# Linear-attention and SwiGLU block, forward and backward: loading the first x tile in two halves and transposing the eighth by DMA

## The chip, the cores and the metric

The kernel runs on one core of one Trainium2 chip. The metric is the device time of one execution in microseconds (us). A NeuronCore has TensorE (PE, matrix products), VectorE (DVE), ScalarE (ACT), GpSimd (POOL) and SyncE (SP); DMAs are issued from the queues of SP, ACT and POOL. "PEld" in a profile is TensorE's weight load, which overlaps its products.

## The reference

With S = 2048 tokens, D = 640, H = 32 heads of 20 and F = 1728, the reference computes the forward pass below and the gradients of its output to x and to all weights:

```
n   = layernorm(x);  q, k, v = split(n @ wqkv)
phi = t -> where(t > 0, t + 1, exp(t)) + 1e-6
o   = (phi(q) (phi(k)^T v)) / (phi(q) . sum(phi(k)) + 1e-6)      per head
h   = x + o @ wo
out = h + (silu(ln(h) @ w_gate) * (ln(h) @ w_up)) @ w_down
```

Only the beginning matters for the change: the layer norm of x and the products for k and q, followed by phi.

## The kernel before

The tokens are cut into 16 tiles of 128 (`ST` = 16). The first stage, which the change concerns, goes over the tiles t = 0 to 15. For each tile DVE computes the row statistics (`ln1_stats`, L268), POOL makes 1/sqrt(var + eps) from them (`ln_rstd`, L137, with two operations, L139 and L140), and DVE writes the normalised copy `xn` (`ln1_xn`, L281). The first `NC` = 3 tiles are only centred (`ln1_centre`, L277), and ACT multiplies by the scale when it reads the product. The product needs `xn` transposed, as `xnT`. For tiles t < `XD` = 8, TensorE transposes it into PSUM in five blocks of 128 columns (`ln1_tr` for tiles 0 and 1, `ln1_tr1` for 2 to 7), and ACT or DVE copies it to SBUF (`copies`, `copy1`; DVE for the tiles in `BY_V`, where they go through `copy1`). For the tiles from `XD` on, SP issues a transposing DMA from `xn` into `xnT` (L378), three tiles ahead of use.

`kq_mm(t, which)` (L299) is the product of tile t for k (`which` = 0) or q (1): ten matmuls of 320 columns, then two reads by ACT, an exp into `pk` or `pqa` and a relu into a ring `rr`. `phi` (L313) joins two tiles of these on DVE in two operations. The tile of PSUM comes from a pool of four slots that all such tiles share by rotation (tag "mm"). A transposed tile is asked for in `between`, after the product's first piece: in the first three products the five blocks of k are taken in `PIECES`, three and then two, so that work can begin on the first three.

Around this, the kernel keeps TensorE busy from the beginning with dummy products of the identity with itself (`warm`, L339: 37 ahead of tile 0's transposes and 8 behind them). Loads are paced: the first statistics release the loads of x tiles 2 and 3 and of w_q (`load_2`), the first copy of tile 0 releases the rest of x and a transposed load of w_down (`load_3`).

The order of this stage is written out by hand: L335 opens a `manual_schedule` that lists all five engines, so each executes its instructions in the order of the program text. On SP this order is: x tile 0, two pieces of w_k, the paced loads, then for each t the transposing DMA of tile t + 3 where there is one, and what the table `queue` (L328) names for t: transposed loads of the output gradient `dh2T` (the first 512 rows at t = 4), and stores of `xnT`, `pk` and `pqa` to DRAM for the backward pass. ACT's queue carries x tile 1. `dh2T` is first used after the products of the stage. Later stages list fewer engines in their `manual_schedule`, and there a planner orders the others by estimated times.

In the loop from L369 the order on DVE for a tile t is: statistics of later tiles, `ln1_xn(t + 3)` where it is for DMA, copies of transposed tiles, then `phi`, then `ln1_xn(t + 2)` for the tiles that TensorE transposes, and at t = `XD` - 4 = 4 the eighth tile's, `ln1_xn(7)`.

The later stages are long sequences of products: key-value sums, attention, the SwiGLU products, and the backward pass.

Of the kernel before, what the change touches and what calls it, by code (L numbers as in the profile page):

```python
# [9 lines left out]
BF16 = mybir.dt.bfloat16  # L10
# [5 lines left out]
P = 128  # L16
# [4 lines left out]
def kernel(  # L21
# [8 lines left out]
    nc = tc.nc  # L30
# [4 lines left out]
    DT = D // P  # L35
# [13 lines left out]
    x_v = A_x.rearrange("b (t p) d -> p (b t) d", p=P)  # L49
# [5 lines left out]
    const = ctx.enter_context(tc.tile_pool(name="const", bufs=1))  # L55
    dram = ctx.enter_context(tc.tile_pool(name="dram", bufs=1, space=bass.MemoryType.DRAM))
    psum = ctx.enter_context(tc.tile_pool(name="psum", bufs=4, space=bass.MemoryType.PSUM))
# [5 lines left out]
    def mm(name):  # L63

        return psum.tile([P, 2, 512], FP32, name=name, tag="mm")

    def row(ps):
        return ps[:, :, :320]

    def half(ap):  # L70
        return ap.rearrange("p (c n) -> p c n", c=2)
# [122 lines left out]
    x_tm = [strips.tile([P, 8, D], BF16, name="x_tm", tag="S") for _ in range(2)]  # L194
# [6 lines left out]
    def load_x(eng, t0, t1):  # L201
        return eng.dma_start(out=x_tm[t0 // 8][:, t0 % 8:(t1 - 1) % 8 + 1, :], in_=x_v[:, t0:t1, :])

    load_x(nc.sync, 0, 1)
    load_x(nc.scalar, 1, 2)
    w_k = A_wqkv[:, D:2 * D].rearrange("(k p) n -> p k n", p=P)
    w_q = A_wqkv[:, 0:D].rearrange("(k p) n -> p k n", p=P)
# [3 lines left out]
    def wait_for(on, dmas):  # L211
        info = mybir.DependencyInfo(mybir.DependencyClass.Sync, mybir.DependencyReason.DATA)
        for dma in dmas:
            tc.add_manual_dep(dma.ins, on.ins.name, info, reason="paced")
# [7 lines left out]
    def load_3():  # L222
        for t0 in range(4, ST, 2):
            yield load_x(nc.sync, t0, t0 + 2)
        yield load_wdT(wdT, 0)
# [11 lines left out]
    with tc.manual_schedule(engines={EngineType.Pool}):  # L237
        ident = const.tile([P, P], BF16, name="ident")
        make_identity(nc, ident[:])
        nhalf = const.tile([P, 4], FP32, name="nhalf")  # L240
        nc.vector.memset(nhalf[:], -0.5)
        ones = const.tile([P, P], BF16, name="ones")
        nc.vector.memset(ones[:], 1.0)
    mask = const.tile([P, 160], BF16, name="mask")
    zb = const.tile([P, D], BF16, name="zb")
    dzb = const.tile([P, D], BF16, name="dzb")
# [13 lines left out]
    xn = big.tile([P, ST, D], BF16, name="xn", tag="B")  # L260
    xnT = big.tile([P, ST, DT, P], BF16, name="xnT", tag="B")
    pk = big.tile([P, ST, D], BF16, name="pk", tag="B")
    pqa = big.tile([P, ST, D], BF16, name="pqa", tag="B")
    NC = 3
    XD = 8
    BY_V = (1, 2, 3)

    def ln1_stats(t):  # L268
        st6 = small.tile([P, 2, 6], FP32, name="st6", tag="st6")
        for ci, (n0, n1) in enumerate(NCH):  # L270
            st = nc.vector.bn_stats(out=st6[:, ci, :], in_=x_tm[t // 8][:, t % 8, n0:n1])
            if t == 0 and ci == 0:
                wait_for(st, load_2())
        nc.vector.bn_aggr(out=mv1[:, t, :], in_=st6[:].rearrange("p a b -> p (a b)"))
        ln_rstd(mv1[:, t:t + 1, :], rstd1, t, 1)

    def ln1_centre(t, c0=0, c1=D):  # L277
        nc.vector.tensor_scalar(out=xn[:, t, c0:c1], in0=x_tm[t // 8][:, t % 8, c0:c1], scalar1=mv1[:, t, 0:1],
                                scalar2=None, op0=ALU.subtract)

    def ln1_xn(t):  # L281
        nc.vector.tensor_scalar(out=xn[:, t, :], in0=x_tm[t // 8][:, t % 8, :], scalar1=mv1[:, t, 0:1],
                                scalar2=rstd1[:, t:t + 1], op0=ALU.subtract, op1=ALU.mult)

    def ln1_tr(t):
        tp = psum.tile([P, 2, 2 * 512], BF16, name="ps_t", tag="mm")
        for c, (k0, k1) in enumerate(((0, 3), (3, DT))):
            for kt in range(k0, k1):
                nc.tensor.transpose(tp[:, c, (kt - k0) * P:(kt - k0 + 1) * P], xn[:, t, kt * P:(kt + 1) * P], ident[:])
        return [(slice(k0, k1), tp[:, c, :(k1 - k0) * P].rearrange("p (k c) -> p k c", c=P))  # L290
                for c, (k0, k1) in enumerate(((0, 3), (3, DT)))]

    def ln1_tr1(t):
        tp = psum.tile([P, D], BF16, name="ps_t", tag="mm")
        for kt in range(DT):
            nc.tensor.transpose(tp[:, kt * P:(kt + 1) * P], xn[:, t, kt * P:(kt + 1) * P], ident[:])
        return tp[:].rearrange("p (k c) -> p k c", c=P)

    def kq_mm(t, which, between=None, pieces=((0, DT),)):  # L299
        dst, w0 = ((pk, D), (pqa, 0))[which]  # L300
        ps = mm("ps_kq")
        for k0, k1 in pieces:
            for ci, (n0, n1) in enumerate(NCH):
                for k in range(k0, k1):
                    nc.tensor.matmul(ps[:, ci, :320], lhsT=xnT[:, t, k, :], rhs=wqk[:, k, w0 + n0:w0 + n1],  # L305
                                     start=(k == 0), stop=(k == DT - 1))
            if between and k0 == 0:
                between()
        sc = rstd1[:, t:t + 1] if t < NC else 1.0
        nc.scalar.activation(out=half(dst[:, t, :]), in_=row(ps), func=ACT.Exp, scale=sc)  # L310
        nc.scalar.activation(out=half(rr[:, 2 * which + t // 2 % 2, t % 2, :]), in_=row(ps), func=ACT.Relu, scale=sc)
# [21 lines left out]
    PIECES = ((0, 3), (3, DT))  # L333

    with tc.manual_schedule(engines={EngineType.PE, EngineType.DVE, EngineType.Activation, EngineType.Pool, EngineType.SP}):  # L335

        ps = mm("ps_warm")

        def warm(n):  # L339
            for _ in range(n):  # L340
                nc.tensor.matmul(ps[:, 0, :P], lhsT=ident[:], rhs=ident[:], start=True, stop=True)  # L341

        def copies(t, eng_copy):
            for sl, src in ln1_tr(t):
                c = eng_copy(out=xnT[:, t, sl], in_=src)
                if t == 0 and sl.start == 0:
                    wait_for(c, load_3())

        def copy1(t):
            (nc.vector.tensor_copy if t in BY_V else nc.scalar.copy)(out=xnT[:, t], in_=ln1_tr1(t))  # L350

        warm(37)
        ln1_stats(0)
        ln1_centre(0, 0, 3 * P)
        ln1_centre(0, 3 * P, D)
        copies(0, nc.scalar.copy)
        warm(8)
        ln1_stats(1)
        ln1_centre(1)
        kq_mm(0, 0, lambda: copies(1, nc.vector.tensor_copy), PIECES)  # L360
        ln1_stats(2)
        ln1_centre(2)
        kq_mm(1, 0, None, PIECES)
        ln1_stats(3)
        kq_mm(0, 1, lambda: copy1(2), PIECES)
        phi(0, 0)
        ln1_xn(3)
        kq_mm(1, 1)
        for t in range(2, ST):  # L369
            if t == 2:  # L370
                ln1_stats(4)
            if t == 4:
                ln1_stats(t + 3)
            if 4 <= t < ST - 4:
                ln1_stats(t + 4)
            if XD <= t + 3 < ST:
                ln1_xn(t + 3)
                nc.sync.dma_start_transpose(out=xnT[:, t + 3], in_=xn[:, t + 3, :])  # L378
            kq_mm(t, 0, (lambda: copy1(t + 1)) if t + 1 < XD else None)
            if t == 2:  # L380
                ln1_stats(5)
            if t == 3:
                ln1_stats(6)
            if t == ST - 1:
                phi(0, t - 1, 1)
            kq_mm(t, 1)
            if t == 3:
                phi(1, 0)
            elif t == ST - 1:
                last_phi = phi(0, t, 1)  # L390
            elif t > 3:
                phi(t % 2, t - 2 - t % 2)
            if t + 2 < XD - 1:
                ln1_xn(t + 2)
            if t == XD - 4:
                ln1_xn(t + 3)
            if ST - NC - 1 <= t < ST - 1:
                ln1_xn(t - ST + NC + 1)
            for f, *a in queue.get(t, ()):
                f(*a)  # L400
# [71 lines left out]
    with tc.manual_schedule(engines={EngineType.PE, EngineType.DVE, EngineType.SP, EngineType.Pool}):  # L472
# [25 lines left out]
        for i in range(DT):  # L498
            ps = mm("ps_y")
            for ci, (n0, n1) in enumerate(NCH):  # L500
                for t in range(ST):
                    nc.tensor.matmul(ps[:, ci, :320], lhsT=xn[:, t, i * P:(i + 1) * P], rhs=pk[:, t, n0:n1],  # L502
                                     start=(t == 0), stop=(t == ST - 1))
# [36 lines left out]
        for i in range(DT):  # L540
            if i % 2 == 0 and i > 0:
                dm(1)
            ps = mm("ps_w2t")
# [15 lines left out]
        for t in range(ST + 2):  # L559
            if t < ST:  # L560
                xr = wk("h1")
                ps = mm("ps_a")
                for ci, (n0, n1) in enumerate(NCH):
                    for i in range(DT):
                        nc.tensor.matmul(ps[:, ci, :320], lhsT=pqsT[:, i, t * P:(t + 1) * P], rhs=W2[:, i, n0:n1],  # L565
                                         start=(i == 0), stop=(i == DT - 1))
# [42 lines left out]
    with tc.manual_schedule(engines={EngineType.SP}):  # L609
# [14 lines left out]
        for g in range(4):  # L624
# [4 lines left out]
            for t in range(0, ST, 2):  # L629
                pg = mm("pg")  # L630
                for c in range(2):
                    for kt in range(DT):
                        nc.tensor.matmul(pg[:, c, :w], lhsT=hnT[:, kt, (t + c) * P:(t + c + 1) * P], rhs=wg[:, kt, 0:w],  # L633
                                         start=(kt == 0), stop=(kt == DT - 1))
                pu = mm("pu")
                for c in range(2):
                    for kt in range(DT):
                        nc.tensor.matmul(pu[:, c, :w], lhsT=hnT[:, kt, (t + c) * P:(t + c + 1) * P],  # L638
                                         rhs=wg[:, kt, w:2 * w], start=(kt == 0), stop=(kt == DT - 1))
# [108 lines left out]
    with tc.manual_schedule(engines={EngineType.SP, EngineType.Pool}):  # L748
# [20 lines left out]
        for t in range(ST + LAG_C):  # L769
            if t < ST:  # L770
# [6 lines left out]
                ps = mm("ps_dhn")  # L777
# [32 lines left out]
            ps = mm("ps_dp")  # L810
# [14 lines left out]
    with tc.manual_schedule(engines={EngineType.SP, EngineType.DVE}):  # L825
# [27 lines left out]
        for i in range(DT):  # L853
            ps = gts.pop(i, None)
            if ps is None:
                ps = mm("ps_gt")
# [57 lines left out]
        ps = mm("ps_dzb")  # L914
# [11 lines left out]
        for t in range(ST + LAG):  # L926
            if t in (2, 3):
                dwqk(0, t + 1)
            if t < ST:
# [5 lines left out]
                ps = mm("ps_dk")  # L935
# [25 lines left out]
            ps = mm("ps_dxn")  # L961
            for ci, (n0, n1) in enumerate(NCH):
                for k, (lhs, rhs) in enumerate(((dqT, wqkvT[:, 0:5]), (pkT, WV2), (dkT, wqkvT[:, 5:10]))):
                    for i in range(DT):
                        nc.tensor.matmul(ps[:, ci, :320], lhsT=lhs[:, i, :], rhs=rhs[:, i, n0:n1],  # L965
                                         start=(k == 0 and i == 0), stop=(k == 2 and i == DT - 1))
# [127 lines left out]
```

## Time and profile before

| what | before |
|---|---|
| time, median of 4 runs | 812.68 us (812.61 to 812.73) |
| time of the profiled execution | 811.96 us |
| its span | 810.2 us |
| TensorE clock granted | 1.0 |
| first dummy product on TensorE | 1.56 us |
| first product of tile 0 (L305) | 6.52 us |
| last product of the k and q stage ends | about 52.2 us |
| transposing DMAs of x tiles (L378) | 8, the first issued at 24.38 us |

Times within the profile count from the start of the span. A line of the timeline gives start and length in us, the engine (with a q for its queue, which issues DMAs), the source line, the operation, what it writes and reads, and in brackets the idle time before it and what ended that. A line of the DMA table gives the destination and source, the queue, the number of DMAs, their size and the median time from the beginning of the issue to the landing. A wait is shown as the engine and line that waited, what it waited for, the total in us, how often, and the longest.

### The profile page before, as it was taken

The numbers are of one execution on the slowest core, as the hardware profiler recorded it, in microseconds if no ns is written. First come the engines' busy times: TensorE is split into PE (matmuls) and PEld (weight loads), VectorE is DVE, ScalarE is ACT, GpSimd is POOL, SyncE is SP. The second block draws the span as 40 slices with busy tenths as digits, with TensorE's granted clock in tenths as the row PEclk, the third lists the DMA queues.
The fourth block names the chain that finished last, engine by engine and source line by source line (L and its number), as shares of the span: only waits on it lengthen the run. The fifth ranks groups of instructions, "written<-read, shape, count | busy, mean of one in ns | idle before, by whom it ended". The sixth has DMA issues, their size and how long they took to land.

```text
span 810.2 us, 13780 instructions
## 1 busy us (share of the span) xinstructions
PE 805.5 (99%) x5436; PEld 518.1 (64%) x5436; DVE 472.9 (58%) x883; ACT 286.1 (35%) x400; POOL 202.0 (25%) x361
## 2 busy tenths in 40 slices
PE   9999999999999999999999999999999999999998
PEld 7776566555555555555666677777777777777676
DVE  7979988880095028810850148999897366631212
ACT  6963532750283035401831122322313133322010
POOL 4600045222522312221225301211221121112330
PEclk9999999999999999999999999999999999999999
DMA  9799899998778978994597767976498869899992
GB/s 258 177 262 277 174 260 245 205 242 201 209 159 201 215 185 187 208 224 94 124 249 162 246 156 212 220 203 168 114 241 167 166 132 171 165 251 223 229 225 78
DMA packets 281904, 159.79 MB, mean 197 GB/s; under 512 B 240220, under 2 KB 267997, under 8 KB 281840
## 3 DMA queue, kind: packets, MB, share of 16 engines
q1 hardware_dynamic: 256912, 83.43, 55.2%
q0 software_dynamic: 18416, 66.95, 26.8%
q10 hardware_dynamic: 6512, 8.54, 3.4%
q8 instruction: 42, 0.69, 0.4%
q14 instruction: 22, 0.18, 0.1%
HBM read 47.68 MB, written 53.66 MB: 125 GB/s over the span
## 4 chain that ended last, share of the span: by engine, by line
PE 99%; POOL 0%; ACT 0%; issue 0%; DVE 0%; POOLq 0%
PE ps_dw L705 22%; PE ps_dhn L109 14%; PE ps_dxn L965 8%; PE ps_o L1023 7%; PE pu L638 7%; PE pg L633 7%; PE ps_kq L305 5%; PE ps_dwqk L888 5%; PE ps_dm L411 5%; PE ps_dk L109 3%; PE ps_gt L763 3%; PE ps_dp L109 3%; PE ps_y L502 3%; PE ps_a L565 3%; PE pdm L411 2%; PE ps_warm L341 1%
## 5 line engine op out<-in xcount | busy, mean ns | idle before, releaser
L109 PE MATMUL ps_dhn<-wgT,cols 128*128 128x320 bf16 x864 | 119.5, 299 | 0.0
L705 PE MATMUL ps_dw<-dd,hn 128*128 128x448 bf16 (+1 forms) x640 | 118.8, 346 | 0.0
L109 PEld LDWEIGHTS <-cols 128*128 128x128 bf16 x864 | 84.5, 98 | 32.9
L705 PEld LDWEIGHTS <-hn 128*128 128x128 bf16 x640 | 62.6, 98 | 54.2
L707 DVE CAST dwev<-ps_dw 128x896 bf16<-128x896 f32 (+3 forms) x12 | 10.9, 908 | 127.2 <-PE ps_dw L705 109.6
L670 POOL DMA_DIRECT2D scr_dT<-stg x64 | 34.8, 543 | 172.3 <-DMA stg<-dd 170.2
L707 ACT CAST dwev<-ps_dw 128x896 bf16<-128x896 f32 (+1 forms) x20 | 17.6, 879 | 160.5 <-PE ps_dw L705 150.5
L147 DVE CUSTOM_DVE_ANT_0 lb_a<-lb_dy,hn 128x640 bf16<-128x640 bf16 x32 | 26.4, 826 | 64.6 <-ACT lb_dy L145 64.6
L633 PE MATMUL pg<-wgu,hnT 128*128 128x448 bf16 (+1 forms) x320 | 63.6, 346 | 0.0
L638 PE MATMUL pu<-wgu,hnT 128*128 128x448 bf16 (+1 forms) x320 | 63.6, 346 | 0.0
L1023 PE MATMUL ps_o<-wd,mT 128*128 128x320 bf16 (+3 forms) x462 | 61.1, 295 | 0.0
L705 PE MATMUL ps_dw<-m_s,dh 128*128 128x448 bf16 (+1 forms) x320 | 60.4, 346 | 0.0
L965 PEld LDWEIGHTS <-ring 128*128 128x128 bf16 x480 | 47.0, 98 | 18.2
L1023 PEld LDWEIGHTS <-mT 128*128 128x128 bf16 (+1 forms) x462 | 41.8, 97 | 17.5 <-issue 2.6
L965 PE MATMUL ps_dxn<-wqkvT,ring 128*128 128x320 bf16 x320 | 51.3, 299 | 0.0
L705 PEld LDWEIGHTS <-dh 128*128 128x128 bf16 x320 | 31.3, 98 | 27.1
L638 PEld LDWEIGHTS <-hnT 128*128 128x128 bf16 x320 | 31.3, 98 | 27.1
L633 PEld LDWEIGHTS <-hnT 128*128 128x128 bf16 x320 | 31.3, 98 | 27.0
L411 PEld LDWEIGHTS <-dh2T 128*128 128x128 bf16 x320 | 31.0, 98 | 25.1
L411 PE MATMUL ps_dm<-wdT,dh2T 128*128 128x448 bf16 (+1 forms) x240 | 46.5, 344 | 0.0
L305 PE MATMUL ps_kq<-wqk,xnT 128*128 128x320 bf16 x320 | 44.9, 299 | 0.1
L145 ACT ACTIVATE lb_dy<-ps_dhn,rstd 128x640 bf16<-128x640 f32 x16 | 12.7, 795 | 85.9 <-PE ps_dhn L109 85.9
(167 smaller groups left out, 1303.9 us busy)
## 6 DMA issues: line engine op xcount, KB each, us to landing
scr_dT<-stg POOLq DMA_DIRECT2D x48, 224.0 KB, 3.3
cols<-scr_dT POOLq DMA_DIRECT2D x6, 1728.0 KB, 8.1
scr_m<-m_s POOLq DMA_DIRECT2D x12, 448.0 KB, 4.7
cols<-scr_dT ACTq DMA_DIRECT2D x2, 1728.0 KB, 10.1
out_dram<-dwev POOLq DMA_DIRECT2D x30, 112.0 KB, 2.5
scr_dT<-stg POOLq DMA_DIRECT2D x16, 192.0 KB, 2.4
scr_pq<-pqa SPq DMA_DIRECT2D x4, 640.0 KB, 4.6
scr_xnT<-xnT SPq DMA_DIRECT2D x4, 640.0 KB, 5.4
```

What stands on the lines that cost most here:

```text
L109: nc.tensor.matmul(ps[:, ci, :320], lhsT=lhs(k), rhs=rhs(k, *NCH[ci]), start=(start and k == 0), stop=(stop and k == n - 1))
L147: nc.vector.tensor_tensor_reduce(out=a[:], in0=dy[:], in1=xhat, scale=1.0, scalar=0.0, op0=ALU.mult, op1=ALU.add, accum_out=sums[:, 1:2])
L305: nc.tensor.matmul(ps[:, ci, :320], lhsT=xnT[:, t, k, :], rhs=wqk[:, k, w0 + n0:w0 + n1], start=(k == 0), stop=(k == DT - 1))
L411: nc.tensor.matmul(ps[:, c, :w], lhsT=dh2T[:, kt, (t + c) * P:(t + c + 1) * P], rhs=wdT[:, kt, o:o + w], start=(kt == 0), stop=(kt == DT - 1))
L633: nc.tensor.matmul(pg[:, c, :w], lhsT=hnT[:, kt, (t + c) * P:(t + c + 1) * P], rhs=wg[:, kt, 0:w], start=(kt == 0), stop=(kt == DT - 1))
L638: nc.tensor.matmul(pu[:, c, :w], lhsT=hnT[:, kt, (t + c) * P:(t + c + 1) * P], rhs=wg[:, kt, w:2 * w], start=(kt == 0), stop=(kt == DT - 1))
L670: nc.gpsimd.dma_start(out=scr_dT[t + c, :, KO[g]:KO[g] + GK[g], :], in_=stg[:, :GK[g], :])
L705: nc.tensor.matmul(ps[:, c, :w], lhsT=lhs(t), rhs=rhs(t), start=(t == 0), stop=(t == ST - 1))
L707: last = copy(out=ev[:, :len(parts), :w], in_=ps[:, :len(parts), :w])
L888: nc.tensor.matmul(ps[:, ci, :320], lhsT=xn_r[:, t, i * P:(i + 1) * P], rhs=dq[t // 8][:, t % 8, n0:n1] if which == 0 else dk[:, t, n0:n1] ...
L965: nc.tensor.matmul(ps[:, ci, :320], lhsT=lhs[:, i, :], rhs=rhs[:, i, n0:n1], start=(k == 0 and i == 0), stop=(k == 2 and i == DT - 1))
L1023: nc.tensor.matmul(po(t, ci), lhsT=mTs[t // 4][r, t % 4, j, :], rhs=wd[r, j, n0:n1], start=(t, ci) not in opened, stop=last)
```

## The change

The first x tile is loaded as two halves of 64 partitions, one from SP's queue and one from ACT's, and x tile 1 follows on ACT's queue. The dummy products use the tile `ones`, which DVE fills as its first operation, in place of the identity, and there are 41 of them ahead of tile 0 instead of 37. `ln1_tr` takes a PSUM tile of its own for each of the two pieces and hands each over before the transposes of the next are issued; it serves tile 0 alone. Tile 1 now goes through `ln1_tr1`, one PSUM tile, and is copied by DVE in the two pieces (`copy_1`). `XD` becomes 7: tile 7, the eighth, is transposed by a DMA from SP, issued at t = 4, ahead of that step's `dh2T` load in SP's order. At t = 4, `ln1_xn(7)` and `ln1_xn(6)` come ahead of `phi`.

```diff
-    load_x(nc.sync, 0, 1)
+    for eng, p0 in ((nc.sync, 0), (nc.scalar, P // 2)):
+        eng.dma_start(out=x_tm[0][p0:p0 + P // 2, 0, :], in_=x_v[p0:p0 + P // 2, 0, :])
     load_x(nc.scalar, 1, 2)
...
         make_identity(nc, ident[:])
+        ones = const.tile([P, P], BF16, name="ones")
+        nc.vector.memset(ones[:], 1.0)
         nhalf = const.tile([P, 4], FP32, name="nhalf")
         nc.vector.memset(nhalf[:], -0.5)
-        ones = const.tile([P, P], BF16, name="ones")
-        nc.vector.memset(ones[:], 1.0)
...
-    XD = 8
+    XD = 7
...
     def ln1_tr(t):
-        tp = psum.tile([P, 2, 2 * 512], BF16, name="ps_t", tag="mm")
-        for c, (k0, k1) in enumerate(((0, 3), (3, DT))):
+        for k0, k1 in PIECES:
+            tp = psum.tile([P, (k1 - k0) * P], BF16, name="ps_t", tag="mm")
             for kt in range(k0, k1):
-                nc.tensor.transpose(tp[:, c, (kt - k0) * P:(kt - k0 + 1) * P], xn[:, t, kt * P:(kt + 1) * P], ident[:])
-        return [(slice(k0, k1), tp[:, c, :(k1 - k0) * P].rearrange("p (k c) -> p k c", c=P))
-                for c, (k0, k1) in enumerate(((0, 3), (3, DT)))]
+                nc.tensor.transpose(tp[:, (kt - k0) * P:(kt - k0 + 1) * P], xn[:, t, kt * P:(kt + 1) * P], ident[:])
+            yield slice(k0, k1), tp[:].rearrange("p (k c) -> p k c", c=P)
...
-                nc.tensor.matmul(ps[:, 0, :P], lhsT=ident[:], rhs=ident[:], start=True, stop=True)
+                nc.tensor.matmul(ps[:, 0, :P], lhsT=ones[:], rhs=ones[:], start=True, stop=True)
...
+        def copy_1():
+            src = ln1_tr1(1)
+            for k0, k1 in PIECES:
+                nc.vector.tensor_copy(out=xnT[:, 1, k0:k1], in_=src[:, k0:k1])
+
...
-        warm(37)
+        warm(41)
...
-        kq_mm(0, 0, lambda: copies(1, nc.vector.tensor_copy), PIECES)
+        kq_mm(0, 0, copy_1, PIECES)
...
                 nc.sync.dma_start_transpose(out=xnT[:, t + 3], in_=xn[:, t + 3, :])
+            if t == XD - 3:
+                ln1_xn(t + 2)
             kq_mm(t, 0, (lambda: copy1(t + 1)) if t + 1 < XD else None)
...
             if t + 2 < XD - 1:
                 ln1_xn(t + 2)
-            if t == XD - 4:
-                ln1_xn(t + 3)
```

## The prediction

> **What bounds the kernel now.** I read the busy times of the page first, then the chain of work that ended last, then the timeline of TensorE in the first 8 us and of the SP queue from 15 to 31 us, then the timeline of VectorE and the landing times of single DMAs.
>
> The page, busy times, and all waits of TensorE in the whole span:
>
> ```profile
> PE 805.5 (99%) x5436; PEld 518.1 (64%) x5436; DVE 472.9 (58%) x883; ACT 286.1 (35%) x400; POOL 202.0 (25%) x361
> ```
>
> ```profile
> PE ps_warm L341 <- POOL ident masks.py:199: 1.6, 1, 1.6
> ```
>
> TensorE (PE) is busy for 805.5 of 810.2 us and has one recorded wait in the whole run, 1.6 us at the start. So time can be won in only two ways here: fewer instructions on TensorE, or an earlier start of its useful work. It can be lost wherever something arrives late for TensorE.
>
> The start in the chain of work (start, length, what):
>
> ```profile
> 1.21 0.30 POOL ident masks.py:199
> 1.52 0.05 issue
> 1.56 4.11 PE ps_warm L341 x37
> 5.67 0.29 PE ps_t L289 x5
> 5.97 0.02 issue
> 5.99 0.49 ACT xnT L345
> 6.48 0.04 issue
> 6.52 0.99 PE ps_kq L305 x6
> ```
>
> The chain runs: identity built, 37 dummy matmuls, five transposes of tile 0, first copy on ACT, first product. The last two are a true chain; between the transposes and the product lies a hole that only the eight further dummy matmuls fill.
>
> The timeline of VectorE (DVE) shows that the data come just in time for the end of the dummies:
>
> ```profile
> 0.87 0.06 DVE L241 MEMSET nhalf<- 128x4 f32 x1 [0.87 <-PEq L1078]
> 0.92 0.17 DVE L243 MEMSET ones<- 128x128 bf16 x1
> ...
> 3.92 0.89 DVE L271 BATCH_NORM_STATS2 st<-x_tm 128x6 f32<-128x320 bf16 x2 [2.83 <-DMA x_tm<-in_A_x_dram]
> ...
> 5.09 0.52 DVE L278 TENSOR_SCALAR xn<-x_tm,mv 128x384 bf16<-128x384 bf16 x2
> ```
>
> Of the 0.52 us at L278 the first piece is some 0.28, so tile 0's first three blocks are ready at about 5.4; the first weight load of L289 is at 5.46. Data and dummies end together: both have to come forward for a gain.
>
> The SP queue:
>
> ```profile
> 16.73 3.16 SPq L228 DMA_TRANSPOSE dh2T<-in_grad_out_dram  x1
> 24.38 2.74 SPq L378 DMA_TRANSPOSE xnT<-xn  x1
> 27.21 0.53 SPq L323 DMA_DIRECT2D scr_pq<-pqa  x1
> 27.84 1.83 SPq L378 DMA_TRANSPOSE xnT<-xn  x1
> 29.72 0.57 SPq L326 DMA_DIRECT2D scr_xnT<-xnT  x1
> 30.38 1.85 SPq L378 DMA_TRANSPOSE xnT<-xn  x1
> ```
>
> SP is free from 19.89 to 24.38, and the DMA engines' share is 0.01 from 21.25 to 25.00. From 24.38 on SP has hardly a gap. That hole is where the added transpose goes.
>
> **What the Trainium skill says.** "TensorE: Matmul & The Clock Gate", Part 1: matmuls of 128 columns take 107 ns apart while the array is cold and 56 warm, and the change comes about 4 us after sustained work begins, with a free-running window, so its moment varies. The trace agrees: 37 in 4.11 us is 111 ns, and the five transposes after them take 0.29 us, 58 ns each. "DMA: Bandwidth & Descriptors", Rules for kernel authors: two transfers to disjoint partition halves share the same engines, "Don't bother". No run here has a split load yet; tile 0 and tile 1, issued at 0.80 and 0.79 on two queues, landed 3.1 and 2.9 us later, side by side, which fits. It means that a gain from the split can only come from tile 1 no longer sharing the engines with tile 0. The same page, DMA Transpose, lets only SP and ACT issue such a transpose; the kernel uses SP alone, so all of them stand in one queue.
>
> **The change part by part.**
> (a) *Dummies on `ones`.* The memset of `ones` (0.17 us) goes ahead of `nhalf`, so it ends near 0.87 + 0.17 = 1.04 and TensorE starts near 1.09 (0.05 after its releaser, as now) in place of 1.56: 0.47 earlier. Four dummies more: 41 x 0.111 = 4.55, end 5.64, that is 0.03 earlier, if all run cold. If the clock opens as long after the start as now (1.56 to about 5.47, 3.9 us), then at 5.0: 35 cold, 6 x 0.057 = 0.34, end 5.34, 0.33 earlier. I take 0.2.
> (b) *Tile 0 in two halves.* Tile 0 alone is 160 KB; at the 312 to 405 GB/s moved from 2.5 us on, 160 KB are 0.4 to 0.5 us. So tile 0 lands up to 0.4 earlier than 3.9, since tile 1 now queues behind it; at worst no earlier, perhaps 0.1 later if half-tile DMAs cost as much as whole ones. I take 0.25. It brings DVE's chain to tile 0 and tile 1 forward by as much and so is the cover that (a) needs. Tile 1 is issued some 0.4 later (one ACT issue is 0.395) and lands near 4.1 to 4.3; its statistics start at 5.52 now, 5.2 then, so that costs nothing.
> (c) *Two PSUM tiles.* The copy of the first three blocks now begins after all five transposes (5.97). With a tile of its own it can begin after three: 2 x 0.057 = 0.11 earlier. The eight dummies behind end 0.29 + 0.45 = 0.74 after the transposes start, the copy 0.17 + 0.02 + 0.48 + 0.04 = 0.71: the gain is 0.10. The rotation of the four PSUM slots gets one more tile here and one less at tile 7; each product still waits for the slot four tiles back, as now: nothing. Tile 1 keeps two copies, from one PSUM tile: nothing.
> (d) *Tile 7 without TensorE.* Five transposes leave the chain: 0.28 us (each such group in the chain is 0.28). The copy on ACT (0.692) goes too, but TensorE never waits for ACT there: nothing on the path.
> (e) *What is moved on DVE.* xn(7) and xn(6) (0.40 each) go ahead of the two operations of phi(k) (0.44 and 0.83), same work in another order. xn(7) needs its rstd from POOL, at 20.40 + 0.57 = 20.97 now, just when DVE gets there (the aggregate ends at 21.00): a wait of at most 0.1. Behind it stand xn(6), needed by transposes at 22.82, which it reaches sooner than now (22.20), and phi(k), whose `rr` buffer is next written past 27: nothing.
> (f) *The SP queue.* The transpose of xn(7) is issued near 21.4 less the 0.3 won before, 21.1. It is needed at the first product of tile 7, at 27.75 now, 27.1 then. Priced as the first of its kind now (2.74 to issue, 4.7 to land) it lands at 25.8: 1.3 to spare. But dh2T's load, issued at 16.73 now, stands behind it in program order: 21.1 + 2.74 + 0.05 = 23.9, and takes 2.7 to 3.2, so that the transpose of xn(8) is issued near 26.7 in place of 24.38. dh2T itself is first used at 60.6. Its place in the queue is the cost.
>
> The landings now against the needs (tile t's first product starts at 27.75 + 2.72 (t - 7)):
>
> ```profile
> xnT<-xn SPq DMA_TRANSPOSE x1, 4.7
> ...
> xnT<-xn SPq DMA_TRANSPOSE x1, 3.9
> ...
> xnT<-xn SPq DMA_TRANSPOSE x1, 4.8
> ```
>
> Tiles 8, 9 and 10 land at 29.1, 31.7 and 35.2, for needs, 0.15 ahead for the weight load, at 30.3, 33.0 and 35.75: slack of 1.2, 1.3 and 0.55. With tile 8 issued at 26.7 and a price of 1.23 to 1.9 (transposes that follow another transpose took 1.23, at tiles 11 and 13), SP is through with it at 27.9 to 28.6 instead of 27.12, so everything behind is 0.8 to 1.5 later. Against this stands that [...] landings seem to lag the data (tile 8's bytes move by 26.5), and that DMA idles at 26.5 to 28.2, so part of the delay is swallowed. Bounds of the lateness on TensorE: 0 if the first issue takes 1.23 and tile 8 starts at 25.2; 2.5 if all take their longest. I take 0 to the forecast, narrowly.
>
> **Sum**: 0.2 (a, covered by b) + 0.1 (c) + 0.28 (d) = 0.55 to 0.6; I count 0.53, as tile 1's data allow TensorE only about what DVE gains. Against the profiled execution (span 810.2, its own time 811.96, so 1.76 around the span) that gives 811.4. The profiled run lies 0.72 under the median of the runs, 812.68; the prediction goes against the median: 812.15. Ends of this case: all-cold dummies and no early landing 812.4; everything full 811.8.
>
> **Rivals.** (1) *dh2T's load in the way*, slower than before: place, SP behind xn(7)'s wait; price, 0.8 to 1.5 later for tiles 8 to 10, less tile 10's slack of 0.55, so 0.25 to 0.95 later than now, with all gains swallowed: about 813.3. It decides from the point where SP finishes tile 8's transpose later than 27.12 + 0.55. Its tail (each issue at its longest: 21.3 + 2.74 + 3.16 + 2.74 = 30.1, 3 late) gives 815. For it: thin slack on three tiles running. Against: the idle DMA engines. (2) *The start gives nothing*: dummies all cold or data no earlier, so only (d) and some of (c) remain: 812.4. The skill's sentence on halves speaks for it. (3) *Another order elsewhere*: where `manual_schedule` doesn't list an engine, a planner orders it by estimated times, which shift; TensorE has no waits to lose, so any change costs: about 813.5, little to go on.
>
> **How the numbers follow.** A difference within 0.2%, 1.6 us, counts as the same: about what a measurement can tell. Forecast 0.50, rival (1) 0.29, rival (2) 0.14, rival (3) 0.07. Over 814.3 come 0.09 of rival (1) and 0.03 of (3): slower 0.12. Under 811.05 would need more than all gains: 0.03. Same 0.85. The range of the likeliest is 811.8 to 812.4; for 8 in 10, with the body of rival (1), 811.8 to 814.1.
>
> **What would show it.** Right: dummies starting near 1.1; statistics of tile 0 near 3.7; the first product near 6.2; no `ps_t` group for tile 7; first product of tile 8 some 0.55 earlier than 30.47 with no wait of TensorE on `xnT`. Wrong: TensorE idle before L305 at tiles 8 to 10, released by a DMA into `xnT`; or the first product not before 6.4.

## The result, and the profile after

The changed kernel takes 814.22 us in the median of 30 runs, the kernel before 812.25 in 49 runs beside it: ratio 1.0026, 95% interval 1.0016 to 1.0037, so about 2.0 us slower. The profiled execution has a span of 812.2 us against 810.2. Half of the runs of the changed kernel lie between 813.39 and 814.41, of the kernel before between 811.93 and 812.58. Single runs lie far above the rest in most kernels, up to 15.5 us above the median (829.82 in dh2_early); they widen the intervals of the ratios and move the ratios off those of the medians, so below the medians are compared, with the middle half of the runs beside them.

All waits of TensorE in the profile after, where there was one before (engine and line, what it waited for, total in us, times, longest):

```profile
PE ps_warm L341 <- DVE nhalf L244: 1.1, 1, 1.1
PE ps_kq L305 <- DMA xnT<-xn: 1.0, 1, 1.0
PE ps_dw L710 <- DMA dh<-in_grad_out_dram: 0.7, 1, 0.7
PE ps_t L296 <- DVE xn L279: 0.2, 1, 0.2
```

The first is the old one, shorter by the earlier start of the dummies. The other three are new. The timeline of TensorE shows the waits at `ps_t` (tile 1) and at `ps_kq`:

```profile
1.11 4.55 PE L341 MATMUL ps_warm<-ones 128*128 128x128 bf16 x41 [1.11 <-DVE nhalf L244]
5.46 0.52 PE L290 MATMUL ps_t<-ident,xn 128*128 128x128 bf16 x5
5.82 0.61 PE L341 MATMUL ps_warm<-ones 128*128 128x128 bf16 x8
6.44 0.99 PE L305 MATMUL ps_kq<-wqk,xnT 128*128 128x320 bf16 x6
7.62 0.45 PE L296 MATMUL ps_t<-ident,xn 128*128 128x128 bf16 x5 [0.19 <-DVE xn L279]
...
23.51 12.39 PE L305 MATMUL ps_kq<-wqk,xnT 128*128 128x320 bf16 x90
36.92 16.47 PE L305 MATMUL ps_kq<-wqk,xnT 128*128 128x320 bf16 x120 [1.01 <-DMA xnT<-xn]
```

The 90 products from 23.51 are q of tile 5 and k and q of tiles 6 to 9, so the product that waits is tile 10's first. There is no transpose of tile 7 between them. Before, everything behind tile 7's transposes ran through without a wait:

```profile
26.23 25.97 PE L305 MATMUL ps_kq<-wqk,xnT 128*128 128x320 bf16 x190
```

The same points in both timelines:

| TensorE reaches | before | after | difference |
|---|---|---|---|
| first product of tile 0 | 6.52 | 6.44 | -0.08 |
| transposes of tile 1 | 7.35 | 7.62 | +0.27 |
| transposes of tile 2 | 10.43 | 10.71 | +0.28 |
| first product of the next stage (`ps_y`) | 52.04 | 53.23 | +1.19 |
| first `ps_dw` product | 172.50 | 173.69 | +1.19 |
| second group of `ps_dw` | 178.56 | 180.66 | +2.10 |
| end of the span | 810.2 | 812.2 | +2.0 |

So the account of this execution is: 0.28 lost at tile 1, 0.28 won by tile 7's transposes, 1.19 lost at tile 10, 0.91 lost where the products wait for the output gradient near 176. The list gives 1.01 for tile 10 because it counts from the end of the product before, and products overlap: each is listed as 0.3 long, but they start 0.14 apart.

VectorE shows why tile 1 is late: its x lands at 6.0, though its load was issued at 1.40. Before, it had landed by 3.7, and VectorE went from tile 0 to tile 1's statistics at 5.52 without a wait.

```profile
3.43 0.89 DVE L272 BATCH_NORM_STATS2 st<-x_tm 128x6 f32<-128x320 bf16 x2 [2.36 <-DMA x_tm<-in_A_x_dram]
...
6.01 0.89 DVE L272 BATCH_NORM_STATS2 st<-x_tm 128x6 f32<-128x320 bf16 x2 [0.90 <-DMA x_tm<-in_A_x_dram]
```

And SP's queue shows the load of dh2T standing between the transposing DMAs of tiles 7 and 8:

```profile
21.76 1.20 SPq L383 DMA_TRANSPOSE xnT<-xn  x1
23.00 2.91 SPq L229 DMA_TRANSPOSE dh2T<-in_grad_out_dram  x1
26.01 1.22 SPq L383 DMA_TRANSPOSE xnT<-xn  x1
27.34 1.41 SPq L323 DMA_DIRECT2D scr_pq<-pqa  x1
28.83 1.93 SPq L383 DMA_TRANSPOSE xnT<-xn  x1
30.82 0.61 SPq L326 DMA_DIRECT2D scr_xnT<-xnT  x1
31.52 1.88 SPq L383 DMA_TRANSPOSE xnT<-xn  x1
```

Tile 8's is issued at 26.01, 1.63 later than before, though xn(8) is written at 24.77 (24.37 + 0.40). Tile 10's is issued at 31.52, 1.14 later than before, and lands 5.4 after its issue where it was 4.8, at 36.9:

```profile
xnT<-xn SPq DMA_TRANSPOSE x1, 5.4
```

The instruction orders of POOL, and of all engines from the second stage on, are the same in both profiles. The planner chose no other order, so rival (3) of the prediction falls.

### The profile page after: what moved, and what is told of

Read it like the earlier page. It is cut to its first block, busy times and chain, and to the rows that moved or that the text cites. A ratio compares the mean times of both kernels' runs of the same rounds, so it can differ in the third digit from the quotient of the medians.

```text
span 812.2 us, 13782 instructions
## 1 busy us (share of the span) xinstructions
PE 806.3 (99%) x5435; PEld 518.1 (64%) x5435; DVE 473.0 (58%) x883; ACT 285.7 (35%) x399; POOL 201.5 (25%) x361
## 3 DMA queue, kind: packets, MB, share of 16 engines
q0 software_dynamic: 18416, 66.95, 26.7%
## 4 chain that ended last, share of the span: by engine, by line
PE 92%; DMA 4%; DVE 3%; issue 0%; ACT 0%; POOL 0%; ACTq 0%; DVEq 0%; POOLq 0%
PE ps_dw L710 21%; PE ps_dhn L109 14%; PE ps_dxn L970 8%; PE ps_o L1028 7%; PE pg L638 6%; PE ps_dwqk L893 5%; PE ps_dm L416 5%; PE pu L643 5%; PE ps_kq L305 3%; PE ps_dk L109 3%; PE ps_gt L768 3%; PE ps_dp L109 3%; PE ps_y L507 3%; PE ps_a L570 3%; DMA stg<-dd 2%; PE pdm L416 2%
## 5 line engine op out<-in xcount | busy, mean ns | idle before, releaser
L1035 DVE TENSOR_TENSOR h1r<-ps_o,h1r 128x640 bf16<-128x640 f32 x15 | 12.1, 823 | 52.6 <-PE ps_o L1028 38.9
```

## The experiments

Theory A: the first dh2T load, which SP's order now puts behind tile 7's transpose, delays the transposes of tiles 8 and following until tile 10 is late. Theory B: the late x tile 1 makes VectorE's chain late, and this reaches tile 10. "Before" is the kernel before in runs on the same chip; it has 812.18 to 812.25 in all of them, so medians are compared across chips too.

| kernel | runs | median | middle half | before | ratio, 95% interval |
|---|---|---|---|---|---|
| changed kernel | 30 | 814.22 | 813.39 to 814.41 | 812.25 | 1.0026 (1.0016 to 1.0037) |
| whole_tile0 | 14 | 813.26 | 812.87 to 813.53 | 812.23 | 1.0003 (0.9988 to 1.0018) |
| dh2T_ahead | 22 | 812.13 | 811.97 to 813.06 | 812.23 | 0.9997 (0.9981 to 1.0013) |
| both_undone | 14 | 811.90 | 811.57 to 812.78 | 812.23 | 0.9999 (0.9986 to 1.0011) |
| tile7_alone | 14 | 813.26 | 812.78 to 814.17 | 812.23 | 1.0012 (1.0000 to 1.0024) |
| start_alone | 13 | 812.32 | 812.12 to 812.64 | 812.18 | 1.0006 (0.9998 to 1.0013) |
| wv_in_its_place | 13 | 812.89 | 812.60 to 813.05 | 812.18 | 1.0017 (1.0001 to 1.0033) |
| dh2T_half | 22 | 811.94 | 811.77 to 812.22 | 812.18 | 1.0006 (0.9990 to 1.0022) |
| after_third | 11 | 813.83 | 813.13 to 814.79 | 812.19 | 1.0013 (0.9989 to 1.0037) |
| dh2_early | 18 | 814.35 | 813.42 to 818.11 | 812.19 | 1.0035 (1.0019 to 1.0051) |
| half_whole | 14 | 811.86 | 811.53 to 812.74 | 812.19 | 1.0004 (0.9991 to 1.0017) |
| half_whole_wq | 14 | 811.97 | 811.40 to 813.27 | 812.19 | 1.0004 (0.9990 to 1.0018) |
| later_dh2T_away | 22 | 813.21 | 813.01 to 813.94 | 812.20 | 1.0026 (1.0009 to 1.0044) |
| half_later_away | 6 | 817.21 | 815.60 to 819.46 | 812.20 | 1.0072 (1.0056 to 1.0087) |

### The parts undone one by one

whole_tile0 undoes the split load in the changed kernel:

```diff
-    for eng, p0 in ((nc.sync, 0), (nc.scalar, P // 2)):
-        eng.dma_start(out=x_tm[0][p0:p0 + P // 2, 0, :], in_=x_v[p0:p0 + P // 2, 0, :])
+    load_x(nc.sync, 0, 1)
```

> The changed kernel with x tile 0 loaded whole from SP, as before; the rest of the change stays. Theory A (the SP queue: the dh2T load stands between tile 7's and tile 8's transposing DMA and makes tile 10 late): tile 1's data land near 3.7 again instead of 6.0 and its transposes are no longer late, 0.28 won, but TensorE still waits about 1.0 for xnT of tile 10, since the order on SP is unchanged: 0.2 to 0.4 under the changed kernel. Theory B (the late x tile 1 makes all of VectorE's chain late, and that is what reaches tile 10): the wait at tile 10 goes too, 1.3 to 1.5 under the changed kernel.

Measured: median 813.26, 0.96 under the changed kernel, between the two theories. VectorE starts tile 1's statistics at 5.55 without a wait. The wait at tile 10 is halved, not gone, and there is one at tile 13 (60 products on); the profiled run, 815.13, is the slowest of the 14:

```profile
36.32 8.32 PE L304 MATMUL ps_kq<-wqk,xnT 128*128 128x320 bf16 x60 [0.52 <-DMA xnT<-xn]
45.69 8.32 PE L304 MATMUL ps_kq<-wqk,xnT 128*128 128x320 bf16 x60 [1.05 <-DMA xnT<-xn]
```

Tile 8's transpose is issued at 25.69, 0.32 earlier than in the changed kernel. So the late tile 1 contributes, but isn't the cause alone. That it does so through VectorE's chain fits the 0.32.

dh2T_ahead keeps the split load and puts the dh2T load where SP issued it before:

```diff
-    queue = {4: [(load_dh2T, 0)], 5: ...
+    queue = {3: [(load_dh2T, 0)], 5: ...
```

> The changed kernel with the first dh2T load put ahead of tile 7's transposing DMA in SP's order, so that it is issued near 17; the split load of tile 0 stays. Theory A: xnT of tile 8 is issued as soon as xn(8) is written, near 24.8 instead of 26.0, the wait at tile 10 is gone, 1.0 to 1.2 under the changed kernel. Theory B: the wait at tile 10 stays at 0.7 or more, no difference over 0.3.

Measured: median 812.13, 2.1 under the changed kernel, as fast as the kernel before. TensorE keeps only the two waits at the start, and on SP nothing stands between tile 7's transpose and tile 8's, which is issued at 24.97:

```profile
PE ps_warm L341 <- DVE nhalf L244: 1.1, 1, 1.1
PE ps_t L296 <- DVE xn L279: 0.2, 1, 0.2
```

```profile
17.05 3.13 SPq L229 DMA_TRANSPOSE dh2T<-in_grad_out_dram  x1
21.93 4.24 SPq L383 DMA_TRANSPOSE xnT<-xn  x2
26.30 0.96 SPq L323 DMA_DIRECT2D scr_pq<-pqa  x1
```

With the load out of the way no loss is left, as theory A has it, and moving one line of SP's order takes back more than tile 10's wait.

both_undone has both edits.

> The changed kernel with tile 0 loaded whole and the first dh2T load ahead of tile 7's transposing DMA. Both theories: no wait of TensorE at tiles 1 and 10, so 0.3 to 0.4 (five transposes and the earlier first product) under the kernel before. If the wait for the output gradient at 176 us is a consequence of the late arrival of TensorE there, it is gone; if it comes and goes from run to run, it may still be there.

Measured: 811.90, 0.33 under the kernel before in the median, an amount that the interval of the ratio doesn't separate from nothing. No wait on `xnT`, none near 176; 0.3 for w_q at 9.7, in an execution whose first product started early, at 6.15.

Four kernels differ only in these two edits. With the load in its place the medians are 814.22 (split x tile 0) and 813.26 (whole); with the load ahead they are 812.13 and 811.90. So the load's place costs 2.1 with the split and 1.4 without it. The split costs 1.0 with the load in its place, and without it 0.2, which isn't clear of the noise. The load is the cause, and the late tile 1 makes it worse by about 1 us, more than the 0.2 to 0.4 that theory A allowed. The dummies, the PSUM tiles and the moved xn(6) and xn(7) are in all four, so none of them makes the loss.

tile7_alone makes only the change to tile 7 in the kernel before:

```diff
-    XD = 8
+    XD = 7
...
+            if t == XD - 3:
+                ln1_xn(t + 2)
             kq_mm(t, 0, (lambda: copy1(t + 1)) if t + 1 < XD else None)
...
-            if t == XD - 4:
-                ln1_xn(t + 3)
```

> The kernel before with the change to tile 7 alone (XD = 7 and the place of xn(6) and xn(7)); start, loads and dummies as before. Theory A: the dh2T load is pushed behind tile 7's transpose, TensorE waits 0.8 to 1.3 at one of tiles 8 to 10, 0.28 is won: 0.5 to 1.0 slower than before. Theory B: no wait, 0.28 faster than before.

Measured: 813.26, 1.03 slower than before in the median, at the upper end of theory A, though the interval of the ratio begins at no difference. The expected wait of 0.8 to 1.3 isn't in the profile: its run, 811.92, is the shortest of the 14, and no wait on `xnT` is listed for the products. Still its 210 products from 23.15 take 29.12, where the same 210 in dh2T_half (below) take 28.69: 0.43 is lost inside, and the chain of work that ended last shows where most of it is. It goes over tile 10's transpose:

```profile
31.00 4.63 DMA xnT<-xn
35.63 0.05 issue
35.68 16.59 PE ps_kq L305 x120
```

start_alone has the changed start and tile 7 on TensorE, as before.

> The kernel before with the changed start alone (split load of tile 0, dummies on ones, two PSUM tiles, tile 1's copy); tile 7 is transposed by TensorE and SP's order is that of before. Theory A: no wait at tile 10; first product about 0.1 earlier, tile 1's transposes 0.2 to 0.3 late because its data land near 6, so 0.1 to 0.4 slower than before. A rival in which the start makes the loss: 0.8 or more slower than before.

Measured: 812.32, 0.14 over the kernel before, with an interval that includes no difference. Tile 1's x lands at 6.03, its transposes start at 7.64, and there is no wait later. The first product isn't earlier in that execution (6.56). The start alone loses next to nothing.

### Issue time on SP, or bytes on the DMA engines

wv_in_its_place has dh2T ahead, and in its old place a plain load of about the same DMA time and a short issue:

```diff
-    queue = {4: [(load_dh2T, 0)], 5: ...
+    queue = {3: [(load_dh2T, 0)], 4: [(load_wv,)], 5: ...
...
-13: [(store_k, 1), (store_x, 2), (load_wv,)],
+13: [(store_k, 1), (store_x, 2)],
```

> The changed kernel with the first dh2T load ahead of tile 7's transpose, and in its old place a plain load of w_v, 800 KB, taken from t = 13. It asks the DMA engines for about as much time (2.3 at 350 GB/s, against 2.26 for 655 KB at 290) but holds SP for about 0.6 in place of 2.9. If SP's issue time is what delays tile 8 and the following: no wait at tile 10, time of dh2T_ahead within 0.3. If the bytes in front of tile 8's on the DMA engines do it: a wait at tiles 8 to 10 of 0.5 or more, 1 us or more over dh2T_ahead.

Measured: 812.89, 0.76 over dh2T_ahead, less than the 1 us expected if the bytes do it; what the load's absence at t = 13 does is in the 0.76 as well. SP is free at 24.19, well ahead of tile 8's issue, and still tile 8's first product waits (this view of TensorE ends at 40 us):

```profile
22.37 1.20 SPq L383 DMA_TRANSPOSE xnT<-xn  x1
23.61 0.58 SPq L232 DMA_DIRECT2D wvo<-in_A_wqkv_dram  x1
25.40 1.20 SPq L383 DMA_TRANSPOSE xnT<-xn  x1
```

```profile
xnT<-xn SPq DMA_TRANSPOSE x1, 6.2
```

```profile
31.61 8.60 PE L305 MATMUL ps_kq<-wqk,xnT 128*128 128x320 bf16 x62 [0.54 <-DMA xnT<-xn]
```

Tile 8's transpose lands 6.2 after its issue, where it was 4.3 in dh2T_ahead. So bytes ahead of it on the DMA engines can delay it by themselves. In this execution the wait at tile 1 was 0.6, but this moved both sides alike: tile 7's first product is at 28.20, 0.44 later than in dh2T_ahead, and tile 8's issue at 25.40, 0.43 later. So the wait at tile 8 isn't the start's.

dh2T_half leaves half of the load in place:

```diff
-    queue = {4: [(load_dh2T, 0)], 5: ...
+    queue = {4: [(load_dh2T, 0, 256)], 5: ...
-12: [(load_dh2T, 1024), ...
+12: [(load_dh2T, 256, 256), (load_dh2T, 1024), ...
```

> The changed kernel with half of the first dh2T load (256 rows) in its place at t = 4 and the other half at t = 12. Theory A: SP is held 1.4 less, tile 8's transpose is issued as soon as xn(8) is there, the wait at tile 10 falls to 0 to 0.3: 1.0 to 2.0 under the changed kernel, unless the added load at t = 12 delays tile 15 or what follows. If it is not the load: no difference over 0.3.

Measured: 811.94, 2.3 under the changed kernel, a little more than expected. Tile 8's transpose is issued at 24.79, and the products run through:

```profile
23.00 1.41 SPq L229 DMA_TRANSPOSE dh2T<-in_grad_out_dram  x1
24.79 1.20 SPq L383 DMA_TRANSPOSE xnT<-xn  x1
```

```profile
23.51 28.69 PE L305 MATMUL ps_kq<-wqk,xnT 128*128 128x320 bf16 x210
```

Half of the load fits in SP's hole, and SP is through with it at 24.41, ahead of tile 8's turn; the whole load held SP until 25.91. This edit halves the issue time and the bytes together, so it doesn't tell them apart.

### The second part of the loss

Two more executions of the changed kernel were profiled, the second with a new set of times.

> The changed kernel unaltered, for one more profile. Theory A: the wait at tile 10 is there again, 0.8 to 1.3. If the wait for the output gradient near 176 belongs to the change it is there again too; if it comes from chance in the DMA traffic it may be absent, or another late wait may stand in its place.

Measured: one run, 814.54, span 812.8. TensorE waits 0.7 at tile 10, 0.6 at tile 1, 0.4 for w_k, none near 176, and 1.3 late in the kernel, at 758 (`ps_dwo`). At tile 10 the list names a read by ACT, which ended 0.06 after tile 10's transpose had landed (36.96); the weight load ahead of the product waited for that landing.

> The changed kernel unaltered, timed beside dh2_early on the same chip, and a third profile. About 2.0 slower than before; a wait of 0.7 to 1.2 at tile 10 in the profile. If the second, late wait (near 176 in one profile, near the end in the other) comes by chance, it stands elsewhere or is absent this time.

Measured: median 813.83, 1.6 over the kernel before and not the 2.0 expected; profiled span 811.3. Tile 10 waits 0.9, tile 1 0.2, and nothing else behind the dummies. So the wait at tile 10 is in all three profiles; the second wait stands in another place each time, or nowhere.

dh2_early takes away what the wait near 176 waited for:

```diff
-            for c in range(4):
-                yield nc.gpsimd.dma_start(out=dh2[:, c * 4:(c + 1) * 4, :], in_=go_v[:, c * 4:(c + 1) * 4, :])
+            for c0, c1 in ((0, 4), (4, 8), (8, 16)):
+                yield nc.gpsimd.dma_start(out=dh2[:, c0:c1, :], in_=go_v[:, c0:c1, :])
```

> The changed kernel with the load of the output gradient for the backward pass (dh2) in three DMAs in place of four, so that its last quarter is issued near 152 with the others and not behind two stores that wait for slow transposes. The wait near 176 can't occur. If that wait makes up what tile 10's wait leaves of the loss: 0.6 to 1.0 under the changed kernel. If it is chance of that one profile: within 0.3 of it.

Measured: 814.35, no gain. That wait doesn't make the median: it is in one of three profiles, and without it nothing is won. The profile has a wait of 0.57 at tile 10 and one of 0.89 at tile 13.

later_dh2T_away keeps the load at t = 4 and moves those of t = 7 and 9:

```diff
-6: [(store_x, 0)], 7: [(load_dh2T, 512, 256)], 8: [(store_x, 1)],
-             9: [(load_dh2T, 768, 256)], 12: [(load_dh2T, 1024),
+6: [(store_x, 0)], 8: [(store_x, 1)],
+             12: [(load_dh2T, 512), (load_dh2T, 1024),
```

> The changed kernel with the dh2T loads of t = 7 and t = 9 taken to t = 12, behind tile 15's transposing DMA; the first load keeps its place at t = 4. The wait at tile 10 stays, 0.7 to 1.2. If the second part of the loss is a further wait within this stage, at tile 13 (seen in two of the profiles, 0.9 and 1.05), it can't occur here: 0.5 to 1.0 under the changed kernel. If that part arises later and by chance, no difference over 0.3.

Measured: 813.21, 1.0 under the changed kernel's 814.22 and 0.6 under the 813.83 of after_third; the ratio's interval doesn't separate it from either. The profile is of a long run (span 819.8, with 6.6 us of waiting near the end), but the stage shows 0.65 at tile 10 and nothing at tile 13. This speaks for tile 13 as the second part in many of the runs. It is not shown: the three profiles of the changed kernel have no wait there, and the difference to after_third, on the same chip, is within the scatter.

### Looking for a better version

half_whole is dh2T_half with tile 0 loaded whole; half_whole_wq also loads w_q's second piece ahead of x tile 3:

```diff
-        yield load_x(nc.sync, 3, 4)
         yield nc.sync.dma_start(out=wqk[:, 3:5, 0:D], in_=w_q[:, 3:5, :])
+        yield load_x(nc.sync, 3, 4)
```

> dh2T_half with x tile 0 loaded whole again: the gain of tile 7's transposes and of the earlier dummies, without the late x tile 1 and without dh2T's load in the way. 0.3 to 0.6 under the kernel before, with no wait of TensorE but one of some 0.3 on w_q near 9.7, as in both_undone.

> half_whole with the second piece of w_q loaded ahead of x tile 3: the wait of 0.3 on w_q goes, x tile 3 lands up to 1 later, which VectorE has about 0.5 of slack for. 0.2 to 0.3 under half_whole if that slack holds, no difference or worse if tile 3's statistics come late.

Measured: 811.86 and 811.97, 0.33 and 0.22 under the kernel before, neither beyond its interval. The first is at the low end of what was expected, without the expected wait for w_q in its profile. The second missed: it was expected 0.2 to 0.3 under the first and lies 0.11 over it. In its profile tile 0's first product is at 6.23 and `ps_y` starts at 51.47, 0.57 earlier than before: 0.28 for tile 7's transposes and 0.29 for a start that was early in that execution. In half_whole's profile, with the first product at 6.74, `ps_y` starts at 51.96, 0.08 earlier. A wait of 2.2 late in the kernel (`ps_dwo`) hides the gain in the second one's run.

half_later_away is dh2T_half with the loads of t = 7 and 9 at t = 12 too.

> dh2T_half with the loads of t = 7 and t = 9 at t = 12 as well. No wait at tiles 8 to 15, as in dh2T_half; with these loads gone tiles 11 to 15 have more slack, so the scatter upward is smaller: median within 0.3 of dh2T_half, 0.1 to 0.4 under the kernel before.

Measured: 817.21, 5.0 slower, a clear miss. The stage has no wait on `xnT`, but SP now issues three dh2T loads from 44.73 to 53.16 and everything behind them later: the transposes of the second stage (L551, L546 before) begin at 90.29 where it was 86.94, and TensorE waits 2.3 at `ps_a`:

```profile
PE ps_a L570 <- ACT dmst L430: 2.3, 1, 2.3
```

The chain behind that wait leads over ACT to SP's transposes of `hn`, the first of which is issued at 124.54 where it was 119.71 in dh2T_half. The profiled run was the shortest of the six, so this is not the whole of the loss.

## Why the prediction was wrong, point by point

The prediction of 812.15 was wrong. Two steps of it failed: that the delay on SP's queue is swallowed (f), and that the later load of x tile 1 costs nothing (b). Its rival (1), given 0.29, named the first of them and the place, tile 10; the size was 2.0 against its 0.6 over before (813.3 against 812.68), and about 1.0 of that comes with the split load, which the rival didn't have.

- **(a) Dummies on `ones`.** The start was right: 1.11 for 1.09. The end was the all-cold one of the two bounds: 41 in 4.55, end 5.66, so nothing won where 0.2 was taken. In other executions the same 41 dummies took 4.30 (both_undone), 4.37 (half_whole_wq) and 3.74 (after_again). That agrees with what the Trainium skill says in "TensorE: Matmul & The Clock Gate", Part 1, of a free-running window, so that the moment of the change varies; I should have counted the gain as a chance, not as a value. Even the luck of after_again won little: its first product waited 0.4 for w_k and came at 6.37.
- **(b) The halves.** Tile 0 landed 0.49 earlier, more than the 0.25 taken, and won nothing, as the dummies ended no earlier. The failed step is "that costs nothing" for tile 1. I took the old landing time, 2.9, for a DMA that is now issued at 1.40, behind a half tile and beside w_k's 800 KB on the same engines: it took 4.6 to land. The Trainium skill says in "DMA: Bandwidth & Descriptors", Issuing engines are not separate DMA queues, that DMAs from different engines run on the same DMA engines and interleave; the 4.6 agrees, and I applied it to tile 0 only. w_k's first piece came later too, 6.0 for 5.2, and that is what after_again's first product waited for. Price: 0.28 on TensorE at tile 1, and a later issue of tile 8's transpose (0.32 earlier in whole_tile0), which with dh2T in the way made about 1 us in the median.
- **(c) Two PSUM tiles.** The first copy came 0.08 earlier and the first product too: 0.08 for 0.10, right in this execution. In after_third, with the transposes at the same 5.46, the first product came at 6.56, no earlier than before.
- **(d) Tile 7.** 0.28 won, no group of transposes; right.
- **(e) VectorE's order.** xn(7) and xn(6) at 21.28, phi(k) behind, no wait that mattered; right.
- **(f) The SP queue.** Here the prediction failed: "Bounds of the lateness on TensorE: 0 ... 2.5 ... I take 0 to the forecast, narrowly." The order of events was right: dh2T behind xn(7), tile 8's issue at 26.01 (26.7 forecast), tile 10 the one that waits. Tile 7's transpose was issued at 21.76, not 21.1, since nothing had been won ahead of it. It held SP for 1.20, not 2.74, and even so the wait came. The failed step is "so part of the delay is swallowed": tile 10's transpose was issued 1.14 later than before and took 5.4 to land, not 4.8, so it landed 1.7 later, against a slack of 0.55, and TensorE lost 1.19. Nor was the end of tile 8's issue the point to decide from, as 27.12 + 0.55 was to be. SP was through with it at 27.23, under that point; the rest of its delay arose behind it, where the store of pqa held SP for 1.41 and not 0.53. Why it did isn't shown: the same store took 1.21 in both_undone, with no load in that place, and 0.49 in wv_in_its_place, behind 800 KB. And the idle DMA engines, which I counted as a reason that the delay is swallowed, are what the load filled: they moved 279 to 290 GB/s from 25.5 to 27.0, where it was 161 falling to 5 before. wv_in_its_place shows that bytes alone can make a landing late. In the changed kernel tile 8 landed 3.9 after its issue, no longer than before, and 1.14 of tile 10's 1.7 are a later issue, so there the time on SP was the larger part.
- **A reading.** The trace of before has tile 7's first product at 27.59, not 27.75, where the ten products ahead of it end: they start 0.136 apart from 26.23. The needs were so taken 0.16 late, and 0.15 was taken off again for the weight load; by the trace tile 10's transpose landed 0.56 ahead of its first product, so the slack of 0.55 stands.
- **The range.** Its top, 814.1, left out the tail of rival (1), which went to 815. Not in it were the split load's share and that a stage with slacks of 0.5 to 1.3 on tile after tile can lose more than once: at tile 10 and, in related kernels, at tile 13.

What stays open: of some 2.0 us, 0.9 to 1.2 at tile 10, from start to start, is in every profile of the changed kernel and falls away when the load is moved. The rest also falls away when the load is moved (dh2T_ahead), so it belongs to the change; that it arises at tile 13 in many runs is what later_dh2T_away suggests, but no profile of the changed kernel itself shows it.

## What to carry to other kernels

When a DMA that waits for data is put into a queue ahead of one that didn't wait, the second is moved to the first one's time: ask what used to be issued in the hole, and count its bytes on the DMA engines as well as its issue time. A landing time read from a profile holds for the traffic of that moment only; a load that is issued 0.6 later behind other loads can land 2.3 later. Where a chain of transfers has slacks of about 1 us on tile after tile, take the smallest slack against the whole delay, and don't count on it being won back.

## What the runs showed of the hardware that was not expected

- The same transposing DMA of one tile (128 x 640) held SP for 1.20 to 2.74 us. The longest was the first one of the kernel before, with the DMA engines idle; the first ones of start_alone and of the changed kernel took 1.20. What makes the difference isn't shown.
- It landed 2.6 to 6.2 us after its issue, by what was ahead of it: 2.6 for tile 7 alone on idle engines, 6.2 behind 800 KB of plain load.
- The 41 dummies at the start took between 3.74 and 4.55 us from one execution to another, with no edit to them or to what releases them.
